# One batch's spectral sum on TensorE, one mask write per head, f32 block sums for three pairs, and an order with a rank per operation

## The chip, the cores and the metric

The kernel runs on one core of one Trainium2 chip. Its time is the device time in microseconds (us) of one launch. Before the change three runs gave 290.68 us as the median, from 289.15 to 290.74 us. A separate run was taken with the hardware profiler: it took 290.12 us, of which the span from the first to the last instruction is 288.2 us.

## What is computed

The inputs are `q`, `k`, `v` of shape 4 x 8 x 768 x 64 (batch, head, position, channel) and two weight matrices, 512 x 2048 and 2048 x 512, all f32. The output is 4 x 768 x 512.

```python
# attention with chosen blocks, per batch and head (block = 64, 12 blocks)
gate = q @ mean_over_block(k).T          # 768 x 12, later blocks excluded
sel  = top 3 of gate, and the own block
attn = softmax(where(sel & causal, q @ k.T / 8, -1e9)) @ v
# heads side by side give x, 768 x 512 per batch
u   = x + real(fft2(x))                  # over positions and channels
un  = (u - mean(u)) / sqrt(var(u) + 1e-6)
out = u + relu(un @ w_ch1) @ w_ch2
```

## The kernel before

Work goes by pairs of heads, 16 in all, four to a batch. `attention(p)` turns one pair into 128 columns of `x`. It loads k, q and v in f32 and makes f16 copies (`_copy`, lines 842 and 843) with the rounding remainders of q (line 598) and k (line 603, into `klo`). TensorE transposes k and q (lines 615 and 681; from pair 7 on DMA transposes do it, lines 623 and 672). `k_sums` adds k over each block by small products: with the flag `sums32` from the f32 data (line 639), else twice from f16, the copy and `klo` (line 644). `spread` (line 661) and `gates` (lines 696 and 701) give the gate scores, VectorE finds the third largest (line 735), compares and gets a 0/1 mask (lines 739 and 753), and `m_turn` (line 760) transposes the mask, two blocks of 128 positions to a 128-column product. `spell` (line 770) writes it as 0 or -60000 into spare rows of the transposed q, in two instructions a head: one for the even and one for the odd blocks, which stand on different partitions. Thus the score product (`scores`, line 793, with a triangle added on line 788) masks itself. ScalarE takes the exponential (line 805), `attend` (line 823) multiplies by v with a column of ones, and lines 832 and 835 divide and write `x`.

`fourier(b)` runs when the four pairs of a batch are there. It folds `x` (lines 855, 866, 876), multiplies by cosine and sine tables (`stage1`, lines 894 and 898), copies the results out (`ty`, `tr`, lines 842 and 843) and multiplies again. For batch 0 that is `stage2`, line 928: four 256-column products for each of six row blocks, after which VectorE adds `x` while it copies the sum from PSUM (line 976). The other batches use a shorter symmetric form (`stage2_half`, lines 934 to 968). Then come mean and variance (983, 986), the square root (994, 998), the normalised rows (1010, 1014) and their transposes (1034 for the first half of batch 0, DMA for the rest). `mlp(b)` has the up products (1137), relu (1149 on ScalarE, 1151 on VectorE) and the down products (1166, with 1172). The last two batches use `down_seven`, a seven-product form with sums on VectorE or GpSimd (line 1061), products on line 1110 and adds on line 1118.

No loop sets the order of the work. Every operation is entered with `P.op`, with a rank, the engines that may do it and a cost for each; `Plan.schedule` (line 153) walks through planned time, lets each engine take the startable operation with the earliest start and then the lowest rank, and the instructions are issued in that order. `Plan.place` (line 144) first replaces every distinct rank between 0 and 30000 by a number of the table `RANKS`, and every earliest time above 59 by one of `RELS`. If TensorE has a planned gap before 75 us, `filler` products without use (line 507) are put there: one for each 0.215 us of the gap less 0.05 us; eleven more stand at the start. The order on each engine, and which engine takes an operation that several may do, are thus fixed when the program is built; on the chip an engine waits at its next instruction. Transfers stand in two queues, SP's (loads, DMA transposes, outputs) and POOL's (weights, small constants).

## Time and profile before

| | |
|---|---|
| median of three runs | 290.68 us |
| profiled execution | 290.12 us |
| its span | 288.2 us |
| TensorE busy | 279.8 us (97%) |
| VectorE busy | 232.8 us (81%) |
| ScalarE busy | 181.7 us (63%) |
| GpSimd busy | 149.0 us (52%) |

In the profile PE is TensorE, PEld its weight loads, DVE VectorE, ACT ScalarE, POOL GpSimd and SP the queue engine; L793 is line 793 of the kernel. "Busy" joins the spans of instructions. A matmul's span reaches over the start of the next, so a busy PE still may have room. PEclk is the granted share of TensorE's clock. The chain of waits follows the work that ended last back to what released it.

### The profile page before, as it was taken

To read this page: it belongs to the slowest core of one execution; us is meant where nothing else is said; L and a number is where in the kernel's file an instruction comes from. 1 tells how busy PE (TensorE), PEld (TensorE's weight loads), DVE (VectorE), ACT (ScalarE), POOL (GpSimd) and SP (SyncE) were. 2 spreads that over 40 slices of the span, in tenths; PEclk is the share of its full clock that TensorE was granted. 3 is DMA by queue.
4 is the path that set the end of the run, shared out by engine and by line. 5 is a ranking of instruction groups with operands and counts; after the bars stand their busy time and mean duration, and the time that the engine had idled before them with its cause. 6 is when DMAs were issued, how large, how long until landed. Compare 5 with 4: busy or idle time off the path is not lost.

```text
span 288.2 us, 8197 instructions
## 1 busy us (share of the span) xinstructions
PE 279.8 (97%) x3006; PEld 196.3 (68%) x3006; DVE 232.8 (81%) x810; ACT 181.7 (63%) x416; POOL 149.0 (52%) x276
## 2 busy tenths in 40 slices
PE   6999999999999999999999999999999999999995
PEld 2768767666755677557765776556686788765884
DVE  5898889799553788996867799999689999257885
ACT  2469999876935497529782887569786601577000
POOL 7467896579777656377974578453001295000000
PEclk9799999999999999999999999999999999999999
DMA  8999999999989999688769993522100122400132
GB/s 203 257 232 219 208 279 207 217 207 191 144 193 204 243 173 232 138 209 177 120 140 238 190 129 91 105 76 75 40 1 2 36 74 99 122 2 0 39 109 73
DMA packets 124055, 41.04 MB, mean 142 GB/s; under 512 B 115704, under 2 KB 120984, under 8 KB 124016
## 3 DMA queue, kind: packets, MB, share of 16 engines
q1 hardware_dynamic: 119536, 35.67, 58.8%
q0 software_dynamic: 3552, 4.56, 9.0%
q8 instruction: 23, 0.38, 0.6%
q10 hardware_dynamic: 928, 0.30, 0.4%
q14 instruction: 16, 0.13, 0.2%
HBM read 28.58 MB, written 6.29 MB: 121 GB/s over the span
## 4 chain that ended last, share of the span: by engine, by line
PE 79%; ACT 9%; DVE 6%; issue 2%; DMA 2%; SPq 0%; ACTq 0%; DVEq 0%
PE bank L1137 29%; PE bank L1166 14%; PE bank L1110 13%; PE bank L793 9%; ACT turned L805 7%; PE bank L823 5%; DMA loads<-in_k_dram 2%; PE bank L894 2%; PE bank L507 1%; PE bank L644 1%; PE bank L681 1%; ACT small L842 1%; DVE turned L770 1%; DVE tr L843 1%; PE bank L696 1%
## 5 line engine op out<-in xcount | busy, mean ns | idle before, releaser
L805 ACT ACTIVATE turned<-bank 128x512 f16<-128x512 f32 (+1 forms) x192 | 89.1, 584 | 23.3 <-PE bank L793 22.3
L1137 PE MATMUL bank<-unT,w 128*128 128x384 f16 x512 | 89.8, 326 | 0.0
L1149 ACT ACTIVATE hT<-bank 128x384 f16<-128x384 f32 x114 | 55.4, 493 | 21.2 <-PE bank L1137 20.1
L1137 PEld LDWEIGHTS <-w 128*128 128x128 f16 x512 | 48.2, 98 | 29.0
L793 PE MATMUL bank<-turned,keys 76*128 76x128 f16 (+7 forms) x384 | 51.3, 258 | 0.5 <-DVE turned L770 0.3
L1166 PE MATMUL bank<-w,hT 128*128 128x512 f16 x192 | 45.7, 379 | 0.0
L793 PEld LDWEIGHTS <-keys 128*128 128x128 f16 (+1 forms) x384 | 29.5, 97 | 12.4 <-issue 0.4
L811 POOL TENSOR_SCALAR_AFFINE_SELECT turned<-turned 128x512 f16<-128x512 f16 (+1 forms) x44 | 21.9, 520 | 17.6 <-ACT turned L805 14.1
L1118 DVE TENSOR_TENSOR u<-u,bank 128x256 f32<-128x256 f32 x72 | 26.2, 416 | 5.5 <-PE bank L1110 4.5
L1166 PEld LDWEIGHTS <-hT 128*128 128x128 f16 x192 | 17.7, 97 | 18.0 <-issue 0.6
L823 PEld LDWEIGHTS <-turned 128*128 128x128 f16 x672 | 23.5, 97 | 6.3 <-ACT turned L805 2.0
L823 PE MATMUL bank<-small,turned 128*128 128x65 f16 x672 | 25.5, 193 | 0.9 <-DVE u L976 0.3
L603 POOL TENSOR_TENSOR loads<-loads 128x384 f16<-128x384 f32 x25 | 22.8, 914 | 5.6 <-DVE u L968 3.3
L1110 PEld LDWEIGHTS <-turned 128*128 128x128 f16 x240 | 23.5, 98 | 2.9
L598 POOL TENSOR_TENSOR turned<-loads,turned 128x320 f16<-128x320 f32 x26 | 20.6, 792 | 8.1 <-DVE small L654 3.2
L770 DVE TENSOR_SCALAR turned<-bank 12x384 f16<-12x384 f16 x64 | 20.3, 316 | 2.7 <-PE bank L760 1.3
L835 DVE TENSOR_TENSOR x<-bank,small 128x384 f16<-128x384 f32 x32 | 17.7, 553 | 0.7
L843 POOL CAST small<-loads 128x384 f16<-128x384 f32 x24 | 12.6, 532 | 9.2 <-DVE pm L866 2.2
L1110 PE MATMUL bank<-loads,turned 128*128 128x256 f16 x144 | 17.0, 273 | 0.0
L983 DVE BATCH_NORM_STATS2 small<-u 128x6 f32<-128x512 f32 x24 | 16.0, 678 | 0.0
L1061 DVE TENSOR_TENSOR turned<-hT 128x384 f16<-128x384 f16 x32 | 11.1, 353 | 5.8 <-ACT hT L1149 5.8
L843 POOL CAST loads<-loads 128x384 f16<-128x384 f32 x24 | 12.1, 507 | 7.1 <-issue 6.1
(139 smaller groups left out, 463.0 us busy)
## 6 DMA issues: line engine op xcount, KB each, us to landing
loads<-in_k_dram SPq DMA_DIRECT2D x28, 192.0 KB, 3.5
loads<-in_v_dram SPq DMA_DIRECT2D x28, 192.0 KB, 3.6
loads<-in_q_dram SPq DMA_DIRECT2D x26, 192.0 KB, 3.6
w<-in_moe_w_ch_dram POOLq DMA_DIRECT2D x16, 256.0 KB, 7.1
out_dram<-u SPq DMA_DIRECT2D x12, 256.0 KB, 3.1
out_dram<-u SPq DMA_DIRECT2D x24, 128.0 KB, 1.7
hT<-in_k_dram SPq DMA_DIRECT2D x4, 192.0 KB, 3.7
hT<-in_q_dram SPq DMA_DIRECT2D x4, 192.0 KB, 4.0
```

Source lines behind the costliest of these rows:

```text
L603: lambda x, n, kh=kh, kl=kl, e=e: eng[x].tensor_tensor(out=kl, in0=kn[a][:, :, e, :], in1=kh, op=OP.subtract),
L770: nc.vector.tensor_scalar(out=rows[:, i::2, :], in0=turned[at:at + NB, 0:3 - i, :], scalar1=-NEG, scalar2=NEG, op0=OP.mult, op1=OP.add)
L793: nc.tensor.matmul(bank32[sp.bank][:, co:co + a1 - a0], KI[e][g3][0:ROWS[e], jt, :], QG[e][g3][0:ROWS[e], a0:a1], start=not added, stop=no ...
L805: lambda x, n, sp=sp, pt=pt, at=at, wid=wid: nc.scalar.activation(out=pt[:, at:at + wid], in_=bank32[sp.bank][:, 0:wid], func=AF.Exp, scal ...
L811: lambda x, n, pt=pt, at=at, nd=nd: nc.gpsimd.affine_select(out=pt[:, at:at + 128 * nd].rearrange("p (a c) -> p a c", a=nd), in_=pt[:, at: ...
L823: nc.tensor.matmul(o[:, st, 0:65], pt[:, col:col + 128], V16[v4][:, e, jt, 0:65], start=(i == 0), stop=(i == 20))
L843: return eng[x].tensor_copy(out=dst, in_=src)
L1110: nc.tensor.matmul(bank32[mp.bank][:, 0:256], lhs[:, z, :], rhs[:, z, :], start=(z == 0), stop=(z == 7))
L1118: lambda x, n, mp=mp, sign=sign, part=part: nc.vector.tensor_tensor(out=part, in0=part, in1=bank32[mp.bank][:, 0:256], op=sign),
L1137: nc.tensor.matmul(bank32[hp_.bank][:, 0:384], w1[:, dt, 128 * it:128 * it + 128], unT[:, dt, 384 * hf:384 * hf + 384], start=(dt == 0), s ...
L1149: nc.scalar.activation(out=o, in_=i_, func=AF.Relu)
L1166: nc.tensor.matmul(bank32[cp.bank], hT[hf][:, it, 128 * j:128 * j + 128], w2[:, it, :], start=(it == 0), stop=(it == NIT - 1))
```

## The change

`stage2` of batch 0 gets two more products a row block, the identity times every second column of `x`, so that PSUM holds the whole sum; what was an add on VectorE is now a copy that ScalarE or VectorE may make. For pairs 0 to 6 `m_turn` transposes one block at a time, five products into 64 partitions in place of three, so that all five blocks of a head stand on the same partitions and `spell` is one instruction of 640 columns. `sums32` holds for pairs 0 to 2 in place of pair 0 alone, so `klo` of pairs 1 and 2 is not made. In batch 0 the fold of line 866 is cut in two column ranges, each of which waits for the pairs that it reads. `place` gives each operation a rank of its own, and `TAKES` binds some 280 operations to one engine. The initial fillers are twelve, and the count of the others leaves out the 0.05 us.

```diff
-    def place(self, ranks, rels):
+    def place(self, ranks, rels, takes):
-        at = dict(zip(sorted({o.rank for o in self.ops if 0 < o.rank < 30000}), ranks, strict=True))
         when = dict(zip(sorted({o.rel for o in self.ops if o.rel > 59.0}), rels, strict=True))
+        for o, rank in zip([o for o in self.ops if 0 < o.rank < 30000], ranks, strict=True):
+            o.rank = rank
         for o in self.ops:
-            o.rank = at.get(o.rank, o.rank)
             o.rel = when.get(o.rel, o.rel)
+        for e, which in takes.items():
+            for i in which:
+                self.ops[i].engs = {e: self.ops[i].engs[e]}
...
-                o.fill = int((st - free[e] - 0.05) / 0.215) if st > 8.0 else 0
+                o.fill = int((st - free[e]) / 0.215) if st > 8.0 else 0
...
+SPELL = 7
...
-    P.op(0, {"PE": 4.9}, lambda x, n: filler(11), r=["warm"], w=["spare"])
+    P.op(0, {"PE": 4.9}, lambda x, n: filler(12), r=["warm"], w=["spare"])
...
-        sums32 = p < 1
+        sums32 = p < 3
...
+        by = 2 if p >= SPELL else 1
+        nj = 6 // by if by == 2 else 5
...
-            for j in range(3):
-                nc.tensor.transpose(bank16[gt.bank][:, 128 * j:128 * j + 128],
-                                    gmp[g2][:, 2 * j:2 * j + 2, :].rearrange("p a c -> p (a c)"),
+            for j in range(nj):
+                nc.tensor.transpose(bank16[gt.bank][0:64 * by, 128 * j:128 * j + 128],
+                                    gmp[g2][:, by * j:by * j + by, :].rearrange("p a c -> p (a c)"),
                                     id16)
...
-                for i in range(2):
+                for i in range(by):
                     at = 64 * i + 32 * e
-                    nc.vector.tensor_scalar(out=rows[:, i::2, :], in0=turned[at:at + NB, 0:3 - i, :],
+                    nc.vector.tensor_scalar(out=rows[:, i::by, :],
+                                            in0=turned[at:at + NB, 0:nj - i, :],
                                             scalar1=-NEG, scalar2=NEG, op0=OP.mult, op1=OP.add)
...
+        parts = ((129, 256, (1, 2)), (1, 129, (0, 1, 3))) if b == 0 else ((1, 256, range(HP)),)
         for i, op in ((0, OP.add), (1, OP.subtract)):
-                      out=pm[:, i, :, 1:256], in0=fsf[:, :, 1:256], in1=fsf[:, :, 511:256:-1],
+            for pi, (d0, d1, hps) in enumerate(parts):
+                          out=pm[:, i, :, d0:d1], in0=fsf[:, :, d0:d1],
+                          in1=fsf[:, :, 512 - d0:512 - d1:-1], op=op),
...
-                                         start=(j == 0), stop=(j == 1))
+                                         start=(j == 0), stop=False)
+                    nc.tensor.matmul(o, id16, X[:, kt, par::2], start=False, stop=True)
...
-                small(base + late + 4, "DVE", 0.61,
-                      lambda x, n, kt=kt, mp=mp: nc.vector.tensor_tensor(
-                          out=U[:, kt, :].rearrange("p (l r) -> p r l", r=2),
-                          in0=bank32[mp.bank].rearrange("p (r l) -> p r l", r=2),
-                          in1=X[:, kt, :].rearrange("p (l r) -> p r l", r=2), op=OP.add),
+                small(base + late + 4, {"ACT": 0.5, "DVE": 0.6}, 0,
+                      lambda x, n, kt=kt, mp=mp: _copy(
+                          x, U[:, kt, :].rearrange("p (l r) -> p r l", r=2),
+                          bank32[mp.bank].rearrange("p (r l) -> p r l", r=2)),
...
-        for o in P.place(RANKS, RELS):
+        for o in P.place(RANKS, RELS, TAKES):
```

The numbers of `RANKS` and `RELS` are all new, so nearly every instruction may stand at another place of its engine's order.

More of the change, by code (lines that the diff above doesn't have):

```diff
@@ L313 @@
 RANKS = [
[47 rows of a table removed]
[151 rows of a table added]
 ]
 RELS = [
-    62.54, 62.957, 66.817, 59.831, 66.014, 61.379, 65.492, 73.715, 77.714, 83.064, 90.589, 97.208,
-    95.24, 107.86, 119.807, 117.558, 127.927, 147.26, 136.922, 143.435, 161.095, 169.656,
-]
+    63.53, 71.66, 50.07, 75.13, 60.96, 65.39, 49.74, 8.25, 37.82, 87.25, 91.17, 49.91, 94.86, 73.52,
+    67.97, 68.3, 14.83, 2.78, 58.79, 53.5, 91.46, 86.96,
+]
+TAKES = dict(
+    ACT=[
[6 rows of a table added]
+    ],
+    DVE=[
[9 rows of a table added]
+    ],
+    POOL=[
[4 rows of a table added]
+    ],
+)
 @with_exitstack
@@ L766, in spell @@
                 rows = QG[e][g3][64 - AT[e]:64 - AT[e] + NB, 128:S].rearrange("p (a c) -> p a c", a=5)
[L767 to L768 removed]
+                turned = bank16[gt.bank][:, 0:128 * nj].rearrange("p (j c) -> p j c", j=nj)
+                for i in range(by):
                     at = 64 * i + 32 * e
[L770 removed]
+                    nc.vector.tensor_scalar(out=rows[:, i::by, :],
+                                            in0=turned[at:at + NB, 0:nj - i, :],
                                             scalar1=-NEG, scalar2=NEG, op0=OP.mult, op1=OP.add)
[L772 removed]
+            small(base + 25, "DVE", 0.69 if by == 2 else 0.47, spell,
                   r=[gt, ("qg", e, g3)], w=[("qm", e, g3)], ps=[gt])
```

27 lines of the change are left out of this document (13 added, 14 removed), and 217 rows, old and new, of tables (ACT, DVE, POOL, RANKS).

## The prediction

> **What bounds the kernel now.** I read the page first, then busy time by stage, then the chain of waits, then VectorE's and ScalarE's rows around the points where a stage ends.
>
> ```profile
> span 288.2 us, 8197 instructions
> PE 279.8 (97%) x3006; PEld 196.3 (68%) x3006; DVE 232.8 (81%) x810; ACT 181.7 (63%) x416; POOL 149.0 (52%) x276
> ```
>
> ```profile
> core 0: us, PE busy (x) PEld busy (x) DVE busy (x) ACT busy (x) POOL busy (x), PEclk, DMA share, GB/s
> 0.00:6.55 6.55, 4.21 (x12) 1.43 (x12) 3.41 (x31) 1.40 (x2) 5.07 (x13) 1.00 0.77 192
> 6.55:17.24 10.69, 10.42 (x128) 7.89 (x129) 9.58 (x37) 4.61 (x10) 4.47 (x7) 0.84 1.15 244
> 17.24:46.04 28.80, 27.90 (x488) 21.49 (x487) 25.18 (x111) 27.96 (x62) 24.13 (x40) 1.00 1.03 234
> 46.04:67.40 21.36, 19.89 (x279) 15.00 (x278) 19.12 (x67) 17.79 (x41) 13.87 (x25) 1.00 1.15 212
> 67.40:285.20 217.80, 217.43 (x2108) 150.47 (x2105) 175.09 (x567) 129.90 (x303) 101.50 (x193) 1.00 0.58 118
> ```
>
> The stages are cut at the first block sum (6.55), the first exponential (17.24), the last write of batch 0's x (46.04), the first up product of the MLP (67.40) and the last product (285.20). From 67.40 on TensorE is busy for 217.43 of 217.80 us. So the end is the time of the first up product, plus the TensorE work that is left then, plus 3.0 us of last add and store. Before 67.40 TensorE is less full than it looks:
>
> ```profile
> core 0: us, PE busy (x) PEld busy (x), PEclk, DMA share, GB/s
> 6.55:17.24 10.69, 4.29 (x13) 1.10 (x13) 0.84 1.15 244
> 17.24:67.40 50.16, 5.94 (x20) 1.73 (x20) 1.00 1.08 225
> ```
>
> These are the fillers alone (L507): 13 and 20 of them. The engines that set the pace there are VectorE up to the first exponential (9.58 of 10.69 us), ScalarE up to 46.04 (27.96 of 28.80) and VectorE again after it.
>
> ```profile
> start us, us, engine line op out<-in xcount [idle before <-releaser]
> 14.92 0.55 DVE L603 TENSOR_TENSOR loads<-hT,loads 128x384 f16<-128x384 f32 x1
> 15.44 1.35 DVE L770 TENSOR_SCALAR turned<-bank 12x384 f16<-12x384 f16 x4
> ...
> 58.07 1.34 DVE L770 TENSOR_SCALAR turned<-bank 12x384 f16<-12x384 f16 x4
> 59.44 1.29 DVE L976 TENSOR_TENSOR u<-bank,x 128x512 f32<-128x512 f32 x2
> 60.64 1.28 DVE L983 BATCH_NORM_STATS2 small<-u 128x6 f32<-128x512 f32 x2
> 61.84 0.16 DVE L986 BATCH_NORM_AGGREGATE small<-small 128x2 f32<-128x6 f32 x1
> 61.92 0.66 DVE L976 TENSOR_TENSOR u<-bank,x 128x512 f32<-128x512 f32 x1
> ```
>
> ```profile
> start us, us, engine line op out<-in xcount [idle before <-releaser]
> 17.24 5.35 ACT L805 ACTIVATE turned<-bank 128x512 f16<-128x512 f32 x12 [2.00 <-PE bank L793]
> ...
> 59.14 4.68 ACT L805 ACTIVATE turned<-bank 128x512 f16<-128x512 f32 x10 [1.52 <-PE bank L793]
> ```
>
> Before both rows of exponentials ScalarE sat idle for scores that waited for mask rows: L770 ran up to 16.79 and 59.41.
>
> **The change, part by part.** TensorE first, by spacing. A row of the chain with n products lasts n-1 spacings and one duration, so each spacing follows from a row and a mean.
>
> ```profile
> 1.33 5.08 DMA loads<-in_k_dram
> 6.55 1.47 PE bank L639 x12
> 65.85 0.85 PE bank L1034 x12
> 112.22 0.45 PE bank L644 x12
> 227.67 15.72 PE bank L1110 x144
> ```
>
> ```profile
> L1110 PE MATMUL bank<-loads,turned 128*128 128x256 f16 x144 | 17.0, 273 | 0.0
> L644 PE MATMUL bank<-small,loads 128*128 128x2 f16 x180 | 6.6, 163 | 0.0
> L1034 PE MATMUL bank<-small,x 128*128 128x128 f16 x12 | 0.8, 219 | 0.2 <-DVE x L1014 0.2
> L639 PE MATMUL bank<-small,loads 128*128 128x2 f32 x12 | 1.5, 250 | 1.0 <-DMA loads<-in_k_dram 1.0
> ```
>
> - x on TensorE: 12 products of 256 columns at (15.72-0.27)/143 = 0.108 us, +1.3 us. No row has a moving operand of every second column. I take the plain spacing, nearest in size; the f32 spacing below is the upper bound, +1.3 also, and below nothing it can't go.
> - f32 sums: a pair has 12 f32 passes at (1.47-0.25)/11 = 0.111, 1.33 us, in place of 12 at (0.45-0.16)/11 = 0.026, 0.31 us. For two pairs +2.0 us.
> - mask: two more transposes a pair at (0.85-0.22)/11 = 0.057, seven pairs, +0.8 us, of which 0.2 for pairs 5 and 6 fall behind the first up product.
>
> Sum +4.1 us, 3.9 of it ahead of the first up product. On the other side the built program has 30 fillers where there were 44: 12, then 8 before the first exponential (13 before) and 10 up to the first up product (20 before). At L507's spacing of about 0.21 us ((1.02-0.38)/3 in the row below) that is about 3.2 us less of filler outside the start. A filler fills a gap and sets no end; fewer of them say that the order has less planned room, not that the chip will keep to it.
>
> ```profile
> 15.74 1.02 PE L507 MATMUL bank<-bsb 128*128 128x512 f16 x4
> ```
>
> VectorE ahead of the first up product, by counts of the built orders:
> - mask writes 24 to 12. A head costs 1.34/2 = 0.67. A write of 640 columns, by the slope of the two forms below, lasts 0.343+256x(0.343-0.290)/128 = 0.45 us. 12 heads x 0.22 = -2.7 us. Bounds for the write: 0.34 (as 384 columns) and 0.67 (no gain).
> - `klo` of pairs 1 and 2: three L603 on VectorE at 0.55 go, -1.6 us, and one on GpSimd (0.91).
> - x adds: four L976 at 0.64 become three plain copies. For a copy of that size from PSUM I take the add's own time, -0.6 us.
> - the fold in halves: four instructions for two, each with half the columns. The cut adds two starts: taken at nothing, at most 2 x 0.2 us by the six-element L832 below.
> - engine choices (two key copies and two `ty` copies more, three `tr` copies fewer, the first rows of pair 6's gate after the up product) come to about nothing.
>
> ```profile
> L770 DVE TENSOR_SCALAR turned<-bank 12x384 f16<-12x384 f16 x32 | 11.0, 343 | 2.0 <-PE bank L760 1.3 <-ACT turned L805 0.2
> L770 DVE TENSOR_SCALAR turned<-bank 12x256 f16<-12x256 f16 x32 | 9.3, 290 | 0.7
> L832 DVE RECIPROCAL small<-bank 128x6 f32<-128x6 f32 x32 | 6.1, 189 | 9.7 <-PE bank L823 8.4 <-PE bank L793 0.8 <-PE bank L661 0.4
> ```
>
> Together about -5 us of some 57. ScalarE gets three copies of 512 columns (about 0.48 each: 12 exponentials in 5.35 us) and loses two key copies: +0.5 us of 51.8.
>
> Now by stage.
> - Up to 6.55: nothing. The k load (5.08 us) ends it. Its two halves change places, and the sums need both; one filler more ends well before.
> - 6.55 to 17.24: -1.0. Between the compare of pair 0's mask and its first scores VectorE did L603 (0.55) and four mask writes (1.35); now L603 is gone and one write (0.45) frees the first head's scores, but a copy of pair 1's keys and one of its q stand there (about 0.5 each), so about -0.4. In the order before, four fillers (1.02 from 15.74) stood between L770's first writes and the first score product; three stand ahead of another product now: -0.8. Against it the f32 sums of pair 1 (1.33) stand ahead of pair 0's gates, which wait for q's copies anyway: +0.2. Bounds: -2.3 (all VectorE relief of the stage) and +1.0 (the sums in full, less the 0.3 they replace).
> - 17.24 to 46.04: -0.4. ScalarE has only 0.84 us of idle time and its work is about the same. Bounds -0.8 (that idle time) and +1.7 (pair 2's sums and three pairs' transposes in full, 1.33+0.34).
> - 46.04 to 67.40: -1.5. VectorE is the bound, and by the orders it has about 2 us less there: mask writes of one pair -0.4, adds -0.6, LN rows to ScalarE -0.5, `tr` copies and fold the rest. Bounds -2.0 and +1.3 (the twelve products of x in full).
> - 67.40 to the end: +0.3, the transposes of pairs 5 and 6. Here the work moves about: 24 more relus on VectorE (0.55 each), 12 more sums of L1061 and 12 more of L964 and L968 on GpSimd (0.91, 0.73). The cover is TensorE, with 42.7 us free on VectorE and 116 on GpSimd; were it gone in the last batch, a sum late by one GpSimd instruction would cost up to 0.9 a time. SP's queue has the tables CS, CDS and SS at its 38th to 43rd place (41st to 43rd before), so they come no later. Of w2's blocks on POOL's queue the fifth is now issued last, after 6.1 us of TensorE work behind the first up product, and the third group of down products, which reads it, stands 16.6 us behind it; the row below gives 7.1 us to land, so some 3 us are left. If that cover goes (GpSimd late by more than 3 us), TensorE waits for the rest. Bounds 0 and +1.8 (two late sums, or as much for w2).
>
> ```profile
> w<-in_moe_w_ch_dram POOLq DMA_DIRECT2D x16, 256.0 KB, 7.1
> ```
>
> Sum -1.0-0.4-1.5+0.3 = -2.6 us. 290.12-2.6 = 287.5 us. The profiled execution lies 0.56 us under the median of the runs shown, 290.68; measured against that, 287.5 is 1.1% less.
>
> [...] The stage before the first exponential holds a stretch at half clock:
>
> ```profile
> 4.70:8.10 3.40, 2.36 (x19) 1.74 (x18) 1.89 (x8) 1.06 (x3) 1.86 (x4) 1.00 1.20 300
> 8.10:11.50 3.40, 3.40 (x30) 2.85 (x30) 2.54 (x7) 1.85 (x4) 1.70 (x2) 0.50 1.17 267
> ```
>
> PEclk is 0.50 from 8.10 to 11.50, after a stretch in which TensorE was busy for 2.36 of 3.40 us. With 14 fillers gone such a stretch could come again between 17 and 67 us. It would double at most 3.4/2 = 1.7 us of work, so +1.7 us at most. I hold it unlikely: with the fillers off and the new products on, TensorE has (47.8-5.9+2.2+2.8)/50.2, 93% busy there (PE busy of the two stages, less 20 fillers, with 10 again and with the new products that fall there).
> [...]
>
> **The rivals.**
> 1. Slower: TensorE sets the pace before the MLP. Place: 17.24 to 67.40, where the fillers hide how full it is. If its waits there stay as long as they are, the new products add up: 290.12+4.1 = 294.3 us. For it speaks that TensorE, VectorE and ScalarE are all above 80% busy there; against it, 33 fillers that carry nothing. It decides once the waits and fillers between 6.55 and 67.40 shrink by less than 4 us.
> 2. No change: the gain is handed back. The first exponential comes 1 us earlier, but ScalarE has the same work, and VectorE's freed time turns into waits for score and sum products. The first up product stays within 0.7 us of 67.4: 290.12+0.3+-0.7, 289.7 to 291.1 us. For it: 0.84 us of idle time on ScalarE in 28.80.
> 3. More: the two waits of ScalarE above (2.00 and 1.52) go as well, beside VectorE's 5 us ahead of the MLP. Then the first up product comes some 6 us earlier: 290.12-6+0.3 = 284.4 us. Against it: the waits change their place more often than they vanish.
> 4. The half clock again: 287.5+1.7 = 289.2 us.
>
> **How the numbers follow.** The forecast holds 0.46, with a range of its own from 285.3 to 289.3 (each stage near its value); rival 1 0.20, rival 2 0.18, rival 3 0.12, rival 4 0.04. A measurement of this kernel can tell about 1% from no change, 2.9 us: faster is below 287.8, slower above 293.6. Faster: 0.30 of the forecast's 0.46 and rival 3, 0.42. Slower: rival 1, except where it is met half way, 0.18. The rest, 0.40, is within 1%. Cases of both signs hold much of the chance, so the range goes from rival 3, less the 0.4 us that TensorE still idles behind 67.40 (284.0), to just short of rival 1's full price (294.0). Left out are half of rival 1, with all upper bounds at once (+5.8, 295.9) beyond it, and the lower end of rival 3, together some 0.15.
>
> **What would show it.** Right: L770 with 14 instructions of 640 columns near 0.45 us; three copies of u on ScalarE; L639 with 36 passes; the first exponential near 16.2, the first up product near 64.5, and no new idle time behind it. Wrong: a first up product at 67 or later with fewer fillers but more TensorE waits ahead of it (rival 1 or 2); new idle time of TensorE after it, at down products that wait for w2 or at L1110 that waits for GpSimd's sums; 256-column products of x with a spacing well above 0.11.

## The result and the profile after

The changed kernel takes 293.19 us as the median of four runs (292.66 to 293.69), the kernel before 290.18 us in four runs taken with them (289.15 to 290.74). The ratio is 1.0108, 95% interval 1.0068 to 1.0147; a run more than 1.5% above the fastest of its kernel counts as slow and is left out of the ratios in this document, but not of the medians. The forecast was 287.5: 1.1% faster was said, 1.1% slower came, inside the range of 284 to 294. The profiled execution took 292.87 us, with a span of 291.2.

The page of the changed kernel, its first lines and the row of the granted clock in 40 slices:

```profile
span 291.2 us, 8195 instructions
...
PE 283.6 (97%) x3018; PEld 200.9 (69%) x3018; DVE 232.4 (80%) x782; ACT 177.7 (61%) x400; POOL 167.6 (58%) x304
...
PEclk9579999999999999999999999999999999999999
```

Busy time by stage, cut at the same five events as before:

```profile
core 0: us, PE busy (x) PEld busy (x) DVE busy (x) ACT busy (x) POOL busy (x), PEclk, DMA share, GB/s
0.00:5.74 5.74, 4.47 (x12) 1.57 (x13) 2.85 (x26) 1.40 (x2) 4.55 (x16) 1.00 0.71 182
5.74:20.02 14.28, 13.28 (x125) 10.66 (x125) 8.21 (x33) 5.40 (x10) 4.86 (x9) 0.64 1.20 257
20.02:49.25 29.23, 28.89 (x496) 23.30 (x495) 24.55 (x105) 28.22 (x62) 21.66 (x36) 1.00 1.03 230
49.25:68.67 19.42, 18.66 (x279) 15.04 (x278) 18.27 (x58) 17.55 (x41) 13.76 (x23) 1.00 0.88 142
68.67:288.03 219.36, 218.34 (x2111) 150.32 (x2110) 178.13 (x564) 125.16 (x287) 122.79 (x223) 1.00 0.60 121
```

| | before | forecast | after |
|---|---|---|---|
| first exponential | 17.24 | -1.0 | 20.02 (+2.8) |
| from there to the last write of batch 0's x | 28.80 | -0.4 | 29.23 (+0.4) |
| from there to the first up product | 21.36 | -1.5 | 19.42 (-1.9) |
| from there to the last product | 217.80 | +0.3 | 219.36 (+1.6) |
| last product | 285.20 | -2.6 | 288.03 (+2.8) |

The third stage gained a little more than was forecast, and the other three lost, the one up to the first exponential most. In the second row of the view TensorE is busy for 13.28 of 14.28 us, but its clock is 0.64. The same view, cut where the clock changes:

```profile
5.09:8.51 3.42, 2.42 (x22) 1.92 (x21) 1.87 (x6) 0.51 (x1) 2.25 (x4) 1.00 1.24 301
8.51:11.92 3.41, 3.41 (x28) 3.32 (x25) 1.63 (x5) 2.00 (x3) 1.05 (x3) 0.50 1.29 248
11.92:15.33 3.41, 3.41 (x46) 3.41 (x47) 2.19 (x16) 1.08 (x3) 2.20 (x4) 0.50 1.28 264
15.33:18.75 3.42, 3.42 (x13) 1.28 (x12) 1.98 (x4) 1.91 (x4) 0.00 (x0) 0.50 1.00 223
```

Where the kernel before has one stretch of 3.4 us at half clock, this one has three in a row, in which TensorE is busy all the time. Its own rows there:

```profile
5.74 1.47 PE L774 MATMUL bank<-small,loads 128*128 128x2 f32 x12
8.21 0.58 PE L750 MATMUL bank<-small,loads 128*128 128x128 f16 x6 [1.00 <-POOL loads L982]
...
10.34 2.56 PE L774 MATMUL bank<-small,loads 128*128 128x2 f32 x12
...
17.07 0.74 PE L898 MATMUL bank<-small,gmp 128*64 128x128 f16 x5
```

The 12 f32 passes of pair 0 (L774) take 1.47 us, those of pair 1, at half clock, 2.56. In front of L750 TensorE waits 1.00 us for pair 0's f16 keys, a copy that GpSimd makes behind several DMA issues.

### The profile page after: what moved, and what is told of

The parts are those of the page before. It is cut to its first block, busy times and chain, and to the rows that moved or that the text cites. A ratio compares the mean times of both kernels' runs of the same rounds, so it can differ in the third digit from the quotient of the medians.

```text
span 291.2 us, 8195 instructions
## 1 busy us (share of the span) xinstructions
PE 283.6 (97%) x3018; PEld 200.9 (69%) x3018; DVE 232.4 (80%) x782; ACT 177.7 (61%) x400; POOL 167.6 (58%) x304
## 4 chain that ended last, share of the span: by engine, by line
PE 81%; ACT 6%; DVE 5%; DMA 4%; issue 1%; POOL 1%; SPq 0%; ACTq 0%; POOLq 0%
PE bank L1281 27%; PE bank L1254 13%; PE bank L1310 12%; PE bank L932 9%; PE bank L962 5%; ACT turned L944 3%; PE bank L1037 2%; DMA turned<-turned 2%; PE bank L816 2%; PE bank L642 1%; PE bank L774 1%; PE bank L898 1%; DMA loads<-in_q_dram 1%; DMA loads<-in_k_dram 1%; PE bank L779 1%
## 5 line engine op out<-in xcount | busy, mean ns | idle before, releaser
L1293 ACT ACTIVATE hT<-bank 128x384 f16<-128x384 f32 x90 | 44.1, 499 | 28.1 <-PE bank L1281 27.7
L1310 PE MATMUL bank<-w,hT 128*128 128x512 f16 x192 | 47.0, 379 | 0.0
L950 POOL TENSOR_SCALAR_AFFINE_SELECT turned<-turned 128x256 f16<-128x256 f16 (+1 forms) x44 | 22.5, 522 | 12.3 <-ACT turned L944 6.2
L1295 DVE TENSOR_SCALAR hT<-bank 128x384 f16<-128x384 f32 x38 | 20.5, 549 | 7.9 <-PE bank L1281 6.7
L1205 POOL TENSOR_TENSOR turned<-hT,hT 128x384 f16<-128x384 f16 x15 | 13.5, 913 | 22.0 <-ACT hT L1293 15.1
L738 POOL TENSOR_TENSOR loads<-loads 128x384 f16<-128x384 f32 x24 | 21.9, 915 | 6.8 <-PE bank L779 1.7
L908 DVE TENSOR_SCALAR turned<-bank 12x384 f16<-12x384 f16 (+2 forms) x50 | 18.2, 364 | 7.5 <-PE bank L898 6.3
L733 POOL TENSOR_TENSOR turned<-loads,turned 128x320 f16<-128x320 f32 x24 | 19.0, 794 | 4.0 <-DVE small L971 1.6
L982 POOL CAST turned<-loads 128x384 f16<-128x384 f32 x26 | 13.0, 507 | 7.6 <-DVE x L1158 2.3
```

The source lines that it names most:

```text
L738: lambda x, n, kh=kh, kl=kl, e=e: eng[x].tensor_tensor(out=kl, in0=kn[a][:, :, e, :], in1=kh, op=OP.subtract),
L950: lambda x, n, pt=pt, at=at, nd=nd: nc.gpsimd.affine_select(out=pt[:, at:at + 128 * nd].rearrange("p (a c) -> p a c", a=nd), in_=pt[:, at: ...
L982: return eng[x].tensor_copy(out=dst, in_=src)
L1293: nc.scalar.activation(out=o, in_=i_, func=AF.Relu)
L1295: nc.vector.tensor_scalar(out=o, in0=i_, scalar1=0.0, scalar2=None, op0=OP.max)
L1310: nc.tensor.matmul(bank32[cp.bank], hT[hf][:, it, 128 * j:128 * j + 128], w2[:, it, :], start=(it == 0), stop=(it == NIT - 1))
```

## The experiments

All were timed beside the kernel before, on one chip for each group of four; its median there was 289.48, 289.75, 289.87 and 289.74 us. The changed kernel was timed earlier, against 290.18. Between groups the ratios are therefore the safer comparison. "exp" is the first exponential, "x" the last write of batch 0's x, "up" the first up product, "rest" the time from there to the last product, all from the profiled run.

| kernel | median us (runs) | ratio to before | exp | x | up | rest |
|---|---|---|---|---|---|---|
| before | | | 17.24 | 46.04 | 67.41 | 217.7 |
| changed | 293.19 (4) | 1.0108 | 20.02 | 49.25 | 68.67 | 219.4 |
| e1_fill | 291.77 (4) | 1.0080, 1.0057 to 1.0104 | 18.41 | 47.61 | 67.02 | 219.6 |
| e2_kfirst | 289.98 (10) | 1.0001, 0.9963 to 1.0039 | 15.44 | 44.66 | 64.06 | 219.5 |
| e3_bf16 | 290.98 (9) | 1.0059, 1.0034 to 1.0084 | 17.39 | 46.41 | 65.83 | 219.5 |
| e4_bf32 | 291.08 (9) | 1.0043, 1.0023 to 1.0063 | 17.70 | 46.92 | 68.30 | 217.7 |
| e5_kfill | 290.17 (12) | 1.0017, 0.9990 to 1.0044 | 17.10 | 46.32 | 65.74 | 219.4 |
| e6_kbf | 292.63 (6) | 1.0096, 1.0064 to 1.0128 | 16.73 | 45.77 | 65.18 | 221.1 |
| e7_two | 293.61 (6) | 1.0103, 1.0070 to 1.0136 | 16.43 | 46.46 | 66.20 | 221.0 |
| e9_wide | 290.48 (12) | 1.0027, 1.0002 to 1.0052 | 16.32 | 45.59 | 65.01 | 222.0 |
| e10_kwide | 290.11 (12) | 1.0004, 0.9984 to 1.0024 | 15.46 | 44.72 | 64.14 | 220.4 |
| e11_bnofill | 290.39 (12) | 1.0016, 0.9997 to 1.0035 | 17.22 | 47.57 | 68.94 | 217.8 |
| e12_kwtwo | 291.24 (12) | 1.0050, 1.0020 to 1.0080 | 15.76 | 45.84 | 65.58 | 222.4 |
| e13_kwlate | 289.00 (12) | 0.9974, 0.9959 to 0.9990 | 15.37 | 44.63 | 64.03 | 220.3 |
| e14_kwx | 292.03 (12) | 1.0067, 1.0038 to 1.0097 | 15.83 | 45.09 | 66.22 | 221.6 |
| e15_kwbf | 289.99 (12) | 1.0011, 0.9991 to 1.0031 | 16.90 | 45.92 | 65.33 | 220.5 |
| e16_late | 292.23 (6) | 1.0087, 1.0066 to 1.0108 | 19.64 | 48.85 | 68.26 | 219.4 |

**First round: what brings the half clock.** e1, on the changed kernel:

```diff
-            P.op(base + 10, {"PE": 0.34}, k_turn, r=...
+            P.op(base + 10, {"PE": 0.34}, lambda x, n: (filler(6 if p == 0 else 0), k_turn(x, n))[1], r=...
```

> The changed kernel with six fillers more, ahead of pair 0's k transposes (L750), where TensorE waits 1.00 us for a k copy; order and engines are otherwise the same. Theory 1, the clock: the changed kernel ran at half clock for three windows (8.50 to 18.75 us) where the one before had a single one, and that moves the first exponential from 17.24 to 20.02. If fillers in that wait keep the clock up, the first exponential comes at 17 to 18 us and the time is 290 to 291 us (ratio to before 1.000 to 1.003). Theory 2, the chain: the waits for copies and the f32 sums of pair 1 set the first exponential whatever the clock; fillers in a wait change nothing, first exponential 20.0, 293.2 us (ratio 1.010).

e2 moves one operation, GpSimd's copy of half of pair 0's keys (number 36), to the 36th place of the order of all engines, ahead of three DMA issues, and takes its wait for VectorE's copy away:

```diff
-        for o in P.place(RANKS, RELS, TAKES):
+        for o in earlier(P.place(RANKS, RELS, TAKES)):
-            if o.hold is not None:
+            if o.hold is not None and o.i != 36:
```

> The changed kernel with GpSimd's copy of pair 0's k (which ended TensorE's wait of 1.00 us) moved ahead of three small DMA issues and without its wait for VectorE's port; all else as it is. Theory 1, the clock: the k transposes follow the sums at once at 7.2 us; TensorE is then active earlier in the window 5.1 to 8.5, and if that keeps the clock up the gain is 2 to 3 us (290.2 to 291.2); if the window stays below its mark, only the wait goes. Theory 2, the chain: 1.0 us less before the first exponential, 292.2 us, the clock as before (0.982).

e3, on the changed kernel, where `half16` takes every second 16-bit word of the f32 data:

```diff
-    kn[a][:, st].rearrange("p e d -> p (e d)"), ind32,
+    half16(kn[a][:, st].rearrange("p e d -> p (e d)")), half16(ind32),
```

> The changed kernel with the block sums of pairs 1 and 2 made from the upper 16 bits of k alone (read as bf16), one pass in place of four-byte passes; so their gate scores are coarser, and the work of the f32 passes is left out for these two pairs. Theory 1, the clock: products of two columns leave the array nearly unused however long they take, and two pairs' f32 passes keep it cold; without them the clock is full one or two windows earlier (granted share 0.988 to 0.994 in place of 0.982), first exponential 17.3 to 18.5, 290.5 to 291.7 us. Theory 2, the chain: the 2.35 us of pair 1's sums shrink to some 0.3, the clock stays at 0.982, the first exponential comes at 18 to 19, 291.5 to 292.5 us.

e4, on the kernel before:

```diff
-                if sums32:
+                if sums32 or p in (1, 2):
```

> The kernel before with f32 block sums for pairs 1 and 2 in place of the two f16 products, at the same places of its order; the remainders of k are still made and not read. Theory 1, the clock: pair 1's sums stand at 12.2 us, after the half-clock window; if such passes let the clock fall again, one or two more windows at half clock follow (granted share 0.988 or 0.982), first exponential 18.5 to 20, 292 to 293 us. Theory 2, the chain: 1.0 us more TensorE work ahead of the first exponential in a stretch that holds fillers, 0 to +1 us, 290.2 to 291.2, granted share 0.994.

e2 came near the forecast up to the first up product in its profile (64.06 us, 64.5 forecast), but not behind it (219.45, 218.1 forecast). It had no half clock before the last product, and these rows:

```profile
core 0: us, PE busy (x) PEld busy (x) DVE busy (x) ACT busy (x) POOL busy (x), PEclk, DMA share, GB/s
6.06:15.44 9.38, 8.70 (x125) 7.25 (x124) 7.81 (x32) 5.09 (x9) 4.52 (x9) 1.00 1.28 261
...
64.06:283.51 219.45, 218.61 (x2111) 150.32 (x2110) 178.01 (x564) 125.11 (x287) 122.41 (x223) 1.00 0.61 121
```

But its ten runs lay apart: 288.1 to 289.1 us in five with a mean clock of 0.998 or more, 290.9 us or more in the five below. e1 left one stretch at half clock in place of three, from 12.88 to 16.30 us, and its fillers held up pair 0's transposes (8.77 us in place of 8.21); its first exponential and its time missed theory 1's ranges. e3, without the f32 passes of two pairs, left two stretches, and its first exponential and its time lie in theory 1's ranges. f32 sums on the order of before (e4) cost 0.46 us at the first exponential and 1.3 us in all, with no stretch at half clock added. So the sums alone are not it, nor the copy alone.

**Second round: gaps, sums, mask, late waits.** All four stand on e2. e5 puts `filler(3 if p == 1 else 0)` ahead of `spread`, e6 is e3's edit, e7 sets `SPELL = 0` with the planned costs kept. e8 moved four products later on TensorE; one pair's gate product came behind its reader, so that the selection of that pair was taken from older numbers. It took 291.74 us (12 runs), with two stretches at half clock in its profile, and tells nothing of the late waits; e13 below takes its place.

> The kernel with pair 0's keys copied first (e2), and three more fillers ahead of the gate sums of pair 1, the place at which TensorE idled 0.68 us at 11.56 in the profile of e2. The e2 runs lay in two groups, 288.1 to 289.1 us at a mean clock of 0.998 or more and 290.9 to 292.0 at 0.994, which is one half-clock stretch of 3.4 us. Theory A (such gaps near the start decide whether a stretch at half clock comes): all runs at 0.998 or more and near 288.5 us, 288.1 to 289.2, 0.5% under the kernel before. Rival (the stretch falls where it falls, fillers at this gap do nothing): both groups come again, median near 290, some runs at 291 or more.

> e2 with the block sums of pairs 1 and 2 from the upper 16 bits of each f32 value of k, one pass each, so their gate scores are coarser; order and all other work as in e2. At the spacings of the profile 24 passes at 0.111 us become 12 at 0.026 or so, 2.3 us less TensorE work ahead of the first up product. Theory A (the f32 sums stand on the path also at full clock): at equal clock 1 to 2 us under e2, 286.5 to 287.5 us where the clock is 0.998 or more. Rival (with the clock full the sums are hidden, their harm was the clock alone): within 0.5 us of e2 at equal clock, 288.1 to 289.1.

> e2 with the mask of pairs 0 to 6 written as in the kernel before: three transposes of two blocks a pair and two writes a head; order and engines as in e2. VectorE has 12 heads more work ahead of the first up product, each 0.67 against 0.50 us, 2.1 us in sum, TensorE 0.6 us less there and 0.8 us in all. Theory A (VectorE's mask writes were on the path, as the forecast had it): first exponential 0.3 us later, first up product about 1 us later, 289 to 290 us at a clock of 0.998 or more. Rival (TensorE is what counts): the same as e2 or up to 0.8 us less, 287.3 to 289.

> e2 with four operations of TensorE behind the first up product put one to three places later in its order: the gates of two pairs, the gate sums of one, and the first product of batch 2's Fourier output, which waited 0.28, 0.17, 0.34 and 0.66 us for VectorE or a DMA transpose. Theory A (behind the first up product TensorE is the bound, so that each such wait is paid in full): the waits shrink from 3.6 to about 2.2 us there, last product minus first up product 218.1 us in place of 219.45, and the time 1.3 us under e2 at equal clock, 286.8 to 287.8 at 0.998 or more. Rival (the wait moves to the next product that needs the same chain): within 0.4 us of e2.

The rival held for e5: the clock fell in 5 of 12 runs (means of 0.987 to 0.994), with the gap filled. In e6 and e7, too, 11 of 12 runs had a mean of 0.987 to 0.994 (each of the two profiles shows a stretch at half clock), so that the prices of sums and mask couldn't be read. This made it worth counting what TensorE did in each stretch. I took from each trace the columns that the matmuls starting in a stretch move (an f32 column counted twice, a choice of mine), as a share of 8,192, a round number near the 8,090 that 3,413 ns hold at the spacing of L1110 before (256 in 0.108 us, 2.37 a nanosecond):

| kernel | share (busy) in the stretch before one at half clock | share (busy) in the stretch before one at full clock, lowest |
|---|---|---|
| before | 0.18 (0.70) | 0.51 (1.00) |
| changed | 0.22 (0.71), 0.26 (1.00), 0.38 (1.00) | 0.45 (1.00) |
| e2 | none | 0.42 (1.00) |
| e5 | 0.36 (1.00) | 0.41 (1.00) |
| e6 | 0.29 (0.60) | 0.44 (0.93) |
| e7 | 0.37 (0.92) | 0.47 (0.92) |

The share of busy time does not order these cases: 1.00 stands on both sides. The share of columns does: 0.38 at most ahead of a half clock, 0.41 at least ahead of a full one.

**Third round: the columns.** The f32 passes stand 0.111 us apart with two columns each. At the rate above 96 columns of f32, counted twice, need an estimated 0.08 us (192/2.37), less than that. So e9 gives them 96, on the changed kernel's own order; the 96-column operand lies in a buffer that is written only later:

```diff
-    unT = sb([128, 4, S], F16, "unT")
+    unT = sb([128, 4, S], F16, "unT"); ind32 = unT[:, 3, 0:192].bitcast(FP)
...
-                    nc.tensor.matmul(bank32[ks.bank][:, 2 * st:2 * st + 2],
+                    nc.tensor.matmul(bank32[ks.bank][:, 2 * st:2 * st + 96],
```

> The changed kernel in its own order; only the moving operand of the f32 sums of pairs 0 to 2 is 96 columns wide in place of two (94 of them zero, written over by the next product or read by nobody). The passes stand at a spacing of 0.111 us whatever they move, and 96 columns need about 0.08 us a pass, so nothing lasts longer; but TensorE now moves columns in that time. Theory A, read off the ten profiles so far: a stretch of 3.41 us is at half clock when TensorE moved fewer than about 0.40 of the columns that it can move at full clock in the stretch before (0.18 to 0.38 in the 13 cases followed by a half, 0.41 to 0.99 in the others), however busy it looked. In the changed kernel the stretch from 5.09 us has 0.23; with 12 wide passes it has about 0.5, and the one with pair 1's sums goes up likewise. So the three stretches at half clock are gone, the first exponential is near 17.3 in place of 20.0, and the time 289.5 to 290.8 us. Rival (the clock goes by busy time or by waits, such as the 1.0 us for pair 0's keys): nothing changes, 292.6 to 293.7 us.

e10 is the same edit on e2, and e12 on e7. e11 is the kernel before with `filler(o.fill if o.start > 17 else 0)`.

> e2 (pair 0's keys copied first) with the f32 sums 96 columns wide. In e2 the first two stretches moved 0.43 and 0.45 of the columns, just over the bound of theory A, so that the place of the stretches decided from run to run. Theory A: with 0.25 more in each, all runs at a clock of 0.998 or more, 288.1 to 289.5 us (waits for the DMA transposes behind the first up product may add up to 1 us). Rival: two groups again, 288.1 to 290.2 at full clock and 290.1 to 293 below it, median 290.

> The kernel before the change without the 13 fillers between its first block sum and its first exponential; the eleven at the start and those behind 17 us stay. Nothing that carries a result is changed. Theory A: the stretch from 8.1 us, now 0.51, goes to about 0.38 and below, so one or two more stretches at half clock follow, first exponential 1 to 2 us later, 291 to 292.5 us. Rival (fillers only fill; the clock does not depend on them): first exponential the same or up to 0.5 us earlier, 289.1 to 290.7 us.

> e7 (pair 0's keys first, mask in two writes a head) with the f32 sums 96 columns wide, so that the clock no longer hides the price of the mask writes. Theory A (VectorE's mask writes stand on the path ahead of the first up product): against e10 the first exponential is 0.3 us and the first up product about 1 us later, 289.2 to 290.5 us. Rival (TensorE is what counts): within 0.4 us of e10.

In e9 and e10 all 24 runs have a mean clock of 0.998 or more; the changed kernel's four had 0.982 to 0.988. This mean counts time without a clock record as full, and records can begin late, as in e11 below. So the two profiles, with records from 5.07 and 4.07 us on, show the full clock outright, the other 22 runs only by their mean. e9 by clock stretches, then by stages, then TensorE's rows:

```profile
5.07:8.48 3.41, 2.44 (x22) 1.91 (x21) 1.86 (x6) 0.51 (x1) 2.24 (x4) 1.00 1.20 291
8.48:11.90 3.42, 3.30 (x57) 3.15 (x55) 1.71 (x5) 2.58 (x5) 1.06 (x3) 1.00 1.20 255
11.90:15.30 3.40, 2.85 (x31) 1.74 (x31) 3.30 (x19) 2.25 (x4) 2.19 (x4) 1.00 1.17 249
```

```profile
5.73:16.32 10.59, 8.95 (x125) 7.34 (x125) 7.86 (x32) 5.33 (x10) 4.83 (x9) 1.00 1.19 261
16.32:45.59 29.27, 28.93 (x496) 23.35 (x495) 24.59 (x105) 28.22 (x62) 21.64 (x36) 1.00 1.05 237
45.59:65.01 19.42, 18.66 (x278) 15.04 (x278) 18.28 (x58) 17.55 (x41) 13.75 (x23) 1.00 1.05 175
65.01:287.00 221.99, 218.71 (x2111) 150.21 (x2110) 178.41 (x564) 125.19 (x287) 122.70 (x223) 1.00 0.60 120
```

```profile
5.73 1.48 PE L774 MATMUL bank<-unT,loads 128*128 128x96 f32 x12
8.19 0.51 PE L750 MATMUL bank<-small,loads 128*128 128x128 f16 x6 [0.97 <-POOL loads L982]
...
9.47 1.47 PE L774 MATMUL bank<-unT,loads 128*128 128x96 f32 x12
...
14.12 0.47 PE L898 MATMUL bank<-small,gmp 128*64 128x128 f16 x5
```

The wait for the keys is still there (0.97), TensorE is as busy in the first stretch (2.44 us against 2.42), the passes take as long (1.48 against 1.47). Only the columns differ: 0.56 of the stretch in place of 0.22. The clock stays full, the first exponential comes at 16.32 in place of 20.02, and the first up product 3.7 us earlier. But the rest takes 2.6 us longer than in the changed kernel in this run (292.05 us, above its median), and over the medians 2.7 us of the 3.7 are kept (2.3 by the ratios).

e10's clock came as theory A had it, its time did not: 290.11 us in place of 288.1 to 289.5, where the five runs of e2 at full clock had taken 288.1 to 289.1 in their group. The two profiles agree up to the first up product (64.14 and 64.06); behind it e10 takes 1.0 us longer. So it is not shown that the wide operand is free for the whole kernel.

e11 kept the clock down, as theory A said: mean 0.982 to 0.988 in 10 of 12 runs, and in the profiled run, whose clock records begin only at 20.68, TensorE's rows have the long spacing from the start (12 f32 passes in 2.56 us, 1.47 before):

```profile
5.96 2.56 PE L639 MATMUL bank<-small,loads 128*128 128x2 f32 x12
...
17.19 2.02 PE L793 MATMUL bank<-turned,keys 128*128 128x128 f16 x8
```

The time hardly followed: +0.16%, with an interval from -0.03 to +0.35, where 291 to 292.5 us were expected. The ten runs took 289.9 to 290.8 us, about as the rival had it; the two others, the profiled one among them, 291.67 and 292.10. In the profile the first exponential stood at 17.22, as before, but the last write of x and the first up product came 1.5 us later. It fits that TensorE has room up to the first exponential in the order of before, where the f16 sums are short (0.46 us in this profile) and VectorE sets the pace; no run shows it. Without those fillers, then, the mean clock was 0.982 to 0.988 in ten of twelve runs, where the kernel before had 0.988 to 1.000 in that group, and the median 0.5 us higher.

e12 against e10: first exponential 0.3 us later, x 1.1 and the first up product 1.4 us later, 1.1 us in the median. Theory A held, with a price above the one it gave (291.24 us, outside 289.2 to 290.5): VectorE's mask writes are on the path.

**Fourth round: what hands the gain back, and the two other parts.** In e10 the products L831, the gates of the later pairs, wait for q's DMA transposes, 1.2 us in all. e13 is e10, and e16 the changed kernel, with seven products one to four places later on TensorE (`later` moves an operation in the list behind the k-th next one of TensorE, and with it whatever reads it or uses its PSUM bank):

```diff
+        for i, k in ((715, 1), (847, 2), (1114, 2), (1182, 4), (1250, 3), (1318, 2), (1390, 1)):
+            behind(o, pe[pe.index(o) + k])
-        for o in earlier(P.place(RANKS, RELS, TAKES)):
+        for o in later(earlier(P.place(RANKS, RELS, TAKES))):
```

> e10 (pair 0's keys first, f32 sums 96 columns wide) with seven operations of TensorE put one to four places later in its order: the gates of five pairs that waited for q's DMA transposes (0.17 to 1.8 us in the profiles of e2, e9 and e10), the gate sums of one pair and the first product of batch 2's Fourier output. All other engines keep their order. Behind the first up product TensorE waits 4.60 us in e10, 2.20 in the kernel before. Theory A (those waits hand back what the start gains): they shrink to 2.0 to 2.8 us, last product minus first up product about 218.3 us in place of 220.4, and the time 288.0 to 288.9 us. Rival (the chain behind those gates, VectorE and the exponentials, is what is late, and the wait only moves to its next product): within 0.5 us of e10, 289.6 to 290.6 us.

> The changed kernel with the seven operations of e13 put later on TensorE and nothing else. Three stretches at half clock stay. Theory A: waits behind the first up product 3.5 to about 2.2 us, last product minus first up product 218.2 in place of 219.4, 291.4 to 292.3 us. Rival: 292.6 to 293.7 us as the changed kernel.

e14, on e10:

```diff
-                                         start=(j == 0), stop=False)
-                    nc.tensor.matmul(o, id16, X[:, kt, par::2], start=False, stop=True)
+                                         start=(j == 0), stop=(j == 1))
...
-                      lambda x, n, kt=kt, mp=mp: _copy(
+                      lambda x, n, kt=kt, mp=mp: nc.vector.tensor_tensor(
```

> e10 without the two identity products a row block in batch 0's Fourier output; VectorE adds x while it copies, as before the change, for all six blocks, three of which ScalarE copied. TensorE has 12 products less (1.3 us), VectorE three 0.64 us adds more. Theory A (VectorE is the bound between x and the first up product): first up product minus last write of x 20.4 to 21.3 us in place of 19.4, time 0.5 to 1.9 us over e10. Rival (TensorE is): 0.5 to 1.3 us under e10.

e15 is e10 with e3's `half16`:

> e10 with the sums of pairs 1 and 2 in bf16 (upper half of each value of k, coarser gate scores), 96 columns wide, one pass each: 12 passes of 0.111 us a pair become six of about 0.04. The clock stays full, as the columns still move (share about 0.1 lower in each stretch). Theory A (the f32 sums cost the path something even at full clock): first exponential 0.5 to 1.1 us before e10's 15.46 and the first up product likewise. Rival (VectorE sets the pace of the start, the sums hide beside it): first exponential within 0.3 us of e10's.

e13 is the one version that beats both kernels, by a quarter of a percent: 0.9974 of the kernel before, interval 0.9959 to 0.9990. It is 1.1 us under e10 by the medians, 0.9 by the ratios, whose intervals just overlap. Its profiled run doesn't show where: TensorE's idle time at L831 is 0.7 us against e10's 1.2, but the rest is 220.29 us, about as long as in e10, where theory A gave 218.3. In e16 TensorE no longer waits at L831, but the rest is 219.40 us, as in the changed kernel (219.36): there the waits only moved. Its median, 292.23, lies in theory A's range and yet can't be told from the changed kernel's 293.19 by these intervals. So by the stage theory A fails for both, and where e13's gain comes from stays open.

e14 by stage, around a new stretch at half clock, and the transposes L1178 ahead of the first up product, in e14 and then in e10:

```profile
45.09:66.22 21.13, 18.06 (x267) 14.27 (x267) 20.07 (x61) 16.11 (x38) 14.10 (x24) 0.96 1.00 176
```

```profile
61.00:64.42 3.42, 1.35 (x28) 1.16 (x25) 3.42 (x11) 1.80 (x4) 0.15 (x1) 1.00 1.14 184
64.42:67.84 3.42, 3.42 (x26) 1.78 (x25) 3.21 (x19) 0.99 (x4) 3.31 (x6) 0.50 0.52 92
```

```profile
63.99 1.31 PE L1178 MATMUL bank<-small,x 128*128 128x128 f16 x12 [2.07 <-ACT x L1154]
```

```profile
62.42 1.10 PE L1178 MATMUL bank<-small,x 128*128 128x128 f16 x12
```

Without x on TensorE the stage takes 21.13 us, not 19.42, and VectorE is busy for all of 61.00 to 64.42 while TensorE moves 0.31 of its columns, after which its clock halves, from L1178 into the first up products. Of the 1.7 us, 1.2 stand ahead of L1178, at full clock (18.90 us after the last write of x in place of 17.70), and 0.5 behind its start, where the clock is halved. Seven of the 12 runs lost clock (means of 0.988 to 0.994, 291.97 to 293.85 us); the five others (0.999 or more) took 289.7 to 290.9, no more than e10. So theory A holds for the stage, and the harm to the whole shows only where the clock falls.

e15: eight runs at full clock, 289.2 to 290.5 us, 0.3 to 0.4 under e10, and four with a mean clock of 0.994, 290.8 to 291.3, where a full clock was expected; the profiled run is one of these (at half clock from 12.21 to 15.62 us, after a stretch in which TensorE moved 0.39 of its columns), so the first exponential can't be compared. By the eight runs the f32 sums cost little at full clock.

## Why the forecast was wrong

**The step that failed is the second stage, "6.55 to 17.24: -1.0", by the clock it was made with.** The kernel before has one stretch at half clock there, and the sum left it at that; the changed kernel has three. Its first exponential came at 20.02 in place of 16.24, which is 3.8 of the 5.4 us by which the last product is later than forecast. e9, the changed kernel with nothing but wider operands, has no stretch at half clock and its first exponential at 16.32, so the three are worth 3.7 us there; its first up product is at 65.01, and 64.5 was forecast. That e9 meets the sum so closely is in part luck, for the sum was made from a kernel with one such stretch. The forecast saw the possibility as rival 4, gave it 0.04 and 1.7 us, and looked for it between 17 and 67 us. It reasoned with busy time ("93% busy there"). Here the clock didn't follow it: in the changed kernel two stretches at 1.00 busy were followed by another at half clock.

**"A filler fills a gap and sets no end" failed with it.** A filler moves 512 columns, 6% of a stretch; an f32 pass of 0.111 us moved two. The change took columns out (13 fillers before the first exponential, 8 after) and put in 1.3 us of passes that move next to none, for 0.3 us. In its one stretch at half clock, busy throughout, the kernel before moved 0.51 and was back at full clock behind it. The changed kernel moved 0.26, then 0.38, and came back only after 0.45.

**The f32 sums** were priced at 2.0 us of TensorE with +0.2 on the path in this stage: e4, with no half clock added, has 0.46 us at the first exponential and 1.3 us in the time.

**"17.24 to 46.04: -0.4"** came out as +0.4. ScalarE is busy for 28.22 of 29.23 us (27.96 of 28.80 before): its work grew by 0.3 us and its idle time from 0.84 to 1.01. The bounds held it. With the mask in two writes the stage is 30.08 us (e12, below), against 29.26 in e10, so the mask gained 0.8 us here, and other parts of the new order, which no run tells apart, lost more.

```profile
15.76:45.84 30.08, 28.63 (x488) 22.94 (x487) 26.62 (x115) 28.48 (x63) 21.62 (x36) 1.00 1.01 228
```

**"46.04 to 67.40: -1.5"** was right: -1.9. x on TensorE is worth 1.2 us of it at full clock (e14), mask writes 0.3 (19.74 in e12 against 19.42).

The counts and durations were right as well. The write of 640 columns was put at 0.45 us and took 0.48, the copies of u on ScalarE took 0.63 for 0.48, and the products of x have the plain duration of 256 columns (276 ns; L1110 before, 273):

```profile
L908 DVE TENSOR_SCALAR turned<-bank 12x640 f16<-12x640 f16 x14 | 6.7, 482 | 3.4 <-PE bank L898 3.0
L1073 PE MATMUL bank<-x,small 128*128 128x256 f16 x12 | 3.3, 276 | 0.0
L981 ACT COPY u<-bank 128x512 f32<-128x512 f32 x3 | 1.9, 628 | 0.8 <-PE bank L1073 0.8
```

**"67.40 to the end: +0.3"** came out as +1.6. The two suspects, w2 and GpSimd's sums, weren't it: no wait of TensorE there is for them. Its idle time went from 0.37 to 1.02 us, most of it at three places. The other 0.9 us lie in its busy time (217.43 to 218.34), 0.3 of them forecast; the rest stays open. Groups of TensorE of the changed kernel, of before, and of e9, and the landing time of q's DMA transposes in the three:

```profile
L831 PE MATMUL bank<-kg,turned 128*128 128x24 f16 x100 | 4.0, 173 | 0.3 <-DMA turned<-turned 0.3
L796 PE MATMUL bank<-small 128*128 128x24 f16 x32 | 3.3, 178 | 0.4 <-DVE small L789 0.4
L1079 PE MATMUL bank<-cds,small 128*128 128x256 f16 x9 | 2.4, 272 | 0.5 <-DVE small L982 0.5
...
turned<-turned SPq DMA_TRANSPOSE x18, 3.6
```

```profile
L696 PE MATMUL bank<-kg,turned 128*128 128x24 f16 x100 | 4.0, 173 | 0.0
...
turned<-turned SPq DMA_TRANSPOSE x18, 3.0
```

```profile
L831 PE MATMUL bank<-kg,turned 128*128 128x24 f16 x100 | 4.1, 173 | 2.6 <-DMA turned<-turned 2.6
...
turned<-turned SPq DMA_TRANSPOSE x18, 3.7
```

Before, the gates never waited for a transpose. In the changed kernel the transposes take 0.6 us more to land in the median, and over the profiles with the new order the gates wait for 0.0 (e16) to 3.0 us (e12). The median doesn't order the waits: it is 3.5 us in e2 with a wait of 0.1, and 3.5 in e10 with 1.2. In e9 one of them is on the chain that ends last, and GpSimd's copy of q stands ahead of it, then three other issues in SP's queue, 2.3 us of them:

```profile
143.16 0.46 POOL turned L982
143.62 0.03 issue
143.65 0.54 SPq L620
...
144.23 1.22 SPq L1170
145.45 0.05 issue
145.51 0.57 SPq L620
...
146.19 1.21 SPq L807
147.40 0.05 issue
147.45 4.79 DMA turned<-turned
```

This is rival 2 at a place where I hadn't looked for it: with the start mended, 1.0 us of e9's gain by the medians (1.4 by the ratios) goes back behind the first up product. The rows show for e9's profiled run that such a wait is on the chain; for the other runs that is argued. Why the transposes land later stays open, and so does whether the earlier start, the wide operand or chance brings the waits: e9's twelve runs, none with a mean clock below 0.998, spread over 4.1 us. An order of SP's queue with q's transposes ahead of the loads wasn't tried.

The change doesn't fail by its parts: up to the first up product the mask writes are worth 1.4 us (e12) and x 1.2 us (e14). It fails by an order that lets TensorE's clock drop and, to a smaller part, by the 1.3 us more than forecast behind the first up product.

## What to carry to other kernels

Before you take work without use, or wide work, off TensorE in a stage that is not full, count the columns it will still move in each 3.4 us: in these traces, up to the last product, shares of 0.391 and less were followed by half a clock, shares of 0.404 and more by a full one, and busy time didn't tell. Where narrow products stand so far apart that wider ones would fit, try a wider moving operand: here 12 passes took 1.48 us with 96 columns and 1.47 with two, the clock stayed full, and the kernel took 2.3 to 2.7 us less. And when a start is mended, look at once whether a queue or a buffer further on takes the gain back.

## What the runs showed of the hardware

In the kernel before the record of half clock lasts 3,413 ns, in the changed kernel 10,240, three times that. Over the profiles of before, after and all sixteen experiments there are 1,469 pairs of neighbouring 3,413 ns stretches of which the first ends ahead of the last product. In the 18 after which the clock was 0.50, TensorE had moved 0.15 to 0.391 of its columns; in the 1,451 after which it was 1.00, 0.404 or more. No pair falls on the other side, whether an f32 column is counted once, twice or four times, though in five of the 18 TensorE was busy for 1.00 of the stretch (to two digits), and in one of the 1,451 for only 0.49. In the stretches that reach past the last product the two sides overlap: in e8 and e14 one with 0.375 was followed by a record of full clock. The 0.40 of e9's theory A was read off ten of these traces, and as it foretold, all 24 runs of e9 and e10 have a mean clock of 0.998 or more.

The first clock record begins at 4.70 us in the kernel before, at 5.09 in the changed kernel, at 4.07 in e10, 5.07 in e9 and 5.38 in e15, and only at 20.68 in e11. e2, with 0.42 and 0.44 in its one profile, took 288.1 us or 292.0. That its stretches began elsewhere in the slower runs is a guess; no trace of a slower run of e2 is there to show it. In the changed kernel the first half clock followed a stretch in which TensorE was busy for 0.71 of the time, the next two stretches without idle time (1.00), and 3.7 us up to the first exponential went with the three.
